# First weight tiles begun from the third attention group on, and Fourier constants queued behind the second batch's local loads

## The chip, the cores and the metric

The kernel runs on one NeuronCore of a Trainium2 chip. The metric is the device time of one execution in microseconds (us); the number for a kernel is the median of its runs. An engine executes its own instructions in order and waits on semaphores for other engines and for DMA transfers. PE is the matrix engine, DVE the vector engine, ACT the scalar engine, POOL is GpSimd, and SP only issues transfers here.

## The reference

```python
attn_out = _attn_ref(q, k, v)              # 4 batches, 8 heads, 576 positions, 64 wide; masks local and strided
x = attn_out.transpose(0, 2, 1, 3).reshape(B, S, H * D)
# first layer
mixed = real(fft(fft(x, axis=1), axis=2))
u = x + mixed
un = (u - mean(u)) / sqrt(var(u) + 1e-6)
x = u + relu(un @ w_ch1) @ w_ch2           # 512 -> 2048 -> 512
# second layer: over tokens, then over channels
u = x + (relu(x.T @ w_tok1) @ w_tok2).T    # 576 -> 256 -> 576
out = u + relu(u @ w_ch1) @ w_ch2          # 512 -> 1536 -> 512
```

The weights come as 64-bit floats.

## The kernel before, in words

**Stages.** Attention of four batches; a Fourier transform of each batch as matrix products with cosine and sine tables (`Fourier`, L254); the first MLP (`Mlp`, matmuls at L379 and L397); the token mixing; the last MLP (L777 and L807). Matrix operands are split into a high and a low part, and a product is three matmuls.

**Attention groups.** `gl` holds 24 groups, numbered by `gno`: six per batch, first three local ones (`gi` 0 to 2), then three strided ones (`gi` 3 to 5). A group's steps are `scores` (mask matmul L175, then q·k at L181, into a bank `sc`), `softmax` (DVE maximum L197, ACT scaling L198, ACT exponentials L200 into `sm`), `trans` (PE transposes L208, ACT copy L210 into `pt`), `av` (L223), and `out` (DVE, then SP writes to `xd` at L243, or L249 and L250).

**Loads of a batch.** q lies in `qz` and k in `k`, one buffer each for the local half (`qz_114`) and the strided half (`qz_115`); v lies in `vl` and `vs`. Batch 0 is loaded from SP. Later batches are loaded from POOL's queue (`bulk`, L142): at `gi == 3` the next batch's local q, k and `vl` (L533, L534), at `gi == 0` the strided q, k and `vs` (L536, L537). A buffer is filled again when the last group of the batch before has read it.

**Constants.** The cosine and sine tables `cs`, `ss`, `cd`, `sd` and `alt` are 13 transfers from POOL's queue (L489 to L493, about 1.7 MB). In the kernel before, a memset (`tick`, L481) waits until `vs` of batch 0 has landed, and the 13 issues follow it.

**Weights.** `load_wa` (L505) takes the next tile of the list `order`: w1 of block 0, w2 of block 0, w1 of block 1 and so on. A tile is a 512 KB load by SP into one of three `wraw` buffers (L86), an ACT step (L90), four DVE steps (L92 to L95) that make 32-bit floats of the 64-bit ones, the high part by ACT (L100) and the low part by POOL (L101). The attention loop calls it eight times. The names below write `wu`, `wAh` and `wAl` for the results.

**Order.** The program is written in the order of the loop, and a list scheduler places every instruction on its engine by the time at which it thinks the operands are there; a call of `load_wa` at a later group can so stand earlier in the queues, and a change of one call moves many neighbours. `tc.issue_after(x)` keeps instructions of a block behind `x` on its engine. Transfers that POOL issues count on eight semaphores in turn (`DMASW0` to `DMASW7`): the ninth waits until the first has landed, and so on.

Of the kernel before, what the change touches and what calls it, by code (L numbers as in the profile page):

```python
# [37 lines left out]
def f32(ap):  # L38
    return ap.bitcast(F32)
# [3 lines left out]
def attention_fourier_mlp_kernel(ctx: ExitStack, tc: tile.TileContext, a: dict, out: bass.AP):  # L43
    nc = tc.nc
# [91 lines left out]
    v_t = {}  # L136

    def bulk(b):
        return nc.gpsimd if b else nc.sync

    def load_qk(b, g, pool):
        t = pool.tile([P, 2, S], F32, tag=f"k{g}", name="k", bufs=(1, 1)[g])  # L142
        k_t[b, g] = t
        for ps in ([slice(0, 1), slice(1, 2)] if b == 0 and g < 1 else [slice(0, 2)]):
            for e in range(2):
                r = slice(64 * e, 64 * e + 64)
                bulk(b).dma_start(out=qz[g][r, e, ps], in_=a["qt"][b, g, r, ps])
            bulk(b).dma_start(out=t[:, ps], in_=a["kt"][b, g, :, ps])

    def load_vl(b):  # L150
        bulk(b).dma_start(out=v_t["l"], in_=a["vl"][b])

    def load_vs(b):
        return bulk(b).dma_start(out=v_t["s"], in_=a["vs"][b])
# [255 lines left out]
    def u_rows(T, u):  # L410
        for p0, n, b, r0 in spans(T):
            nc.sync.dma_start(out=u[p0:p0 + n], in_=ud[b][r0:r0 + n, :])
        return u
# [5 lines left out]
    def ln_stats(us, pool, prev=None):  # L419
        n = len(us)  # L420
        mv = pool.tile([P, 3, 4], F32, tag="mv", name="mv", bufs=2)
        for i, u in enumerate(us):
            st = pool.tile([P, 6], F32, tag="bs", name="bs", bufs=2)
            behind(nc.vector.bn_stats(out=st, in_=u), prev)
            nc.vector.bn_aggr(out=mv[:, i, 0:2], in_=st)
        behind(nc.scalar.activation(out=mv[:, :n, 2], in_=mv[:, :n, 1], func=AF.Sqrt, bias=eps), gl[-1].exp)
        nc.vector.reciprocal(out=mv[:, :n, 3], in_=mv[:, :n, 2])
        nc.vector.scalar_tensor_tensor(out=mv[:, :n, 2], in0=mv[:, :n, 0], scalar=-1.0, in1=mv[:, :n, 3],
                                       op0=ALU.mult, op1=ALU.mult)
        return [mv[:, i] for i in range(n)]  # L430
# [9 lines left out]
    if True:  # L440
# [23 lines left out]
        for g in range(2):  # L464
            for hp in range(2):
                nc.vector.memset(qz[g][64:128, 0, hp], 0.0)
                nc.vector.memset(qz[g][0:64, 1, hp], 0.0)
        load_vl(0)
        load_qk(0, 1, ap)
        vlast = load_vs(0)  # L470
        for b in range(B):
            nc.sync.dma_start(out=xd[b][S // 2:S // 2 + 1], in_=zero)

        cs = [fp.tile([P, 3, 290], F32R, name=f"cs{i}") for i in range(2)]
        ss = [fp.tile([P, 3, 290], F32R, name=f"ss{i}") for i in range(2)]
        cd = [fp.tile([P, 2, 258], F32R, name=f"cd{i}") for i in range(2)]
        sd = [fp.tile([P, 2, 258], F32R, name=f"sd{i}") for i in range(2)]
        alt = fp.tile([P, 258], F32R, name="alt")
        f = fp.tile([P, 2, 3, 512], F32R, name="f")
        g4 = [fp.tile([P, 290], F32R, name=f"g4{x}") for x in "hl"]  # L480
        tick = nc.gpsimd.memset(f32(g4[0]), 0.0)  # L481
        tc.add_manual_dep(tick.ins, vlast.ins.name, mybir.DependencyInfo(mybir.DependencyClass.Sync, mybir.DependencyReason.DATA), reason="constants behind the first batch")
        for t in (g4[1], alt, f[:, 0, 2], f[:, 1, 2], cs[0][:, 2], cs[1][:, 2], ss[0][:, 2], ss[1][:, 2]):
            nc.gpsimd.memset(f32(t), 0.0)
        cons = tc.issue_after(tick.ins)
        cons.__enter__()
        for i in range(2):
            for t, w in ((cs[i], a["cs"][i]), (ss[i], a["ss"][i])):
                nc.gpsimd.dma_start(out=t[:, 0:2], in_=w[:, 0:2])  # L489
                nc.gpsimd.dma_start(out=t[:33, 2], in_=w[:33, 2])  # L490
            nc.gpsimd.dma_start(out=cd[i], in_=a["cd"][i])
            nc.gpsimd.dma_start(out=sd[i], in_=a["sd"][i])
        nc.gpsimd.dma_start(out=alt[:2], in_=a["alt"])  # L493
        cons.__exit__(None, None, None)

        fst2 = ExitStack()
        fq = fst2.enter_context(tc.tile_pool(name="fft2", bufs=1, side="left"))
# [7 lines left out]
        def load_wa():  # L505
            if order:
                x, f = order.pop(0)
                pool, tag = (wa, "wa") if f < 4 else (wx, "wx") if f < 8 else (wb, "wb") if f < 12 else (wc, "wc")
                (w1 if x == "1" else w2)[f] = slot_w(a["w1a" if x == "1" else "w2a"][f], pool, tag, "wA")

        def fft(b):

            four_b, n = four[b], 6 * (b + 1)
            d = 1 if b == 0 else 0
            for i in range(3):
                g, e = divmod(7 + d + i, 2)
                yield n + g, lambda i=i, p=(n + g, e): four_b.prep(i, group(*p, "red"))
            for mt in range(5):
                p = (n + 5 + (mt + d) // 2, (mt + d) % 2)
                yield p[0], lambda mt=mt, p=p: four_b.s1(mt, group(*p, "mm"))  # L520
            for i in range(3):
                p = (n + 7 + (i + d + 1) // 2, (i + d + 1) % 2)
                yield p[0], lambda i=i, p=p: four_b.s2(i, group(*p, "mm"))
# [6 lines left out]
        for gno, g in enumerate(gl):  # L530
            b, gi = g.b, g.gi
            if gi == 3 and b + 1 < B:
                load_qk(b + 1, 0, ap)  # L533
                load_vl(b + 1)  # L534
            if gi == 0 and b > 0:
                load_qk(b, 1, ap)  # L536
                load_vs(b)  # L537
            g.scores()
            for e in range(2):
                g.softmax(e)  # L540
            for e in range(2):
                g.trans(e)
            for e in range(2):
                g.av(e)
                g.out(e)
            if gi == 2 and b > 0:
                for i in range(3):
                    four[b - 1].load(i)
                slices += fft(b - 1)
            while slices and slices[0][0] <= gno:  # L550
                slices.pop(0)[1]()
            if gno == 19:
                us = [u_rows(T, lp.tile([P, DM], F32, tag="u", name="u", bufs=6)) for T in range(3)]
            if gno == 23:
                mvs = ln_stats(us, lp, gl[21].red[1])
            if gno >= 8 and gno % 2 == 0:
                load_wa()
        for _, piece in slices:
            piece()
# [410 lines left out]
```

## Time and profile before

| | |
|---|---|
| median of 3 runs | 956.71 us (955.11 to 959.26) |
| the profiled execution | 954.82 us, span of its instructions 953.0 us |
| busy: PE, PEld, DVE, ACT, POOL | 97%, 89%, 57%, 39%, 23% of the span |
| matmuls | 6094 |
| moved by DMA | 113.86 MB, mean 119 GB/s |
| granted TensorE clock, mean | 0.994 of full speed |

A row of a timeline has the start in us, the duration in us, engine, line, operation, the tile written and read, the shape, and in brackets the idle time of the engine before it with what ended it. PEld is the loading of weights into PE, which overlaps PE. The attention of the four batches takes about the first 150 us.

### The profile page before, as it was taken

How to read it: one execution, taken by the hardware profiler on the slowest of the kernel's cores; microseconds unless marked ns; L12 is line 12 of the kernel's file. 1: busy time of each engine (PE TensorE's matmuls, PEld its weight loads, DVE VectorE, ACT ScalarE, POOL GpSimd, SP SyncE). 2: the span in 40 equal slices, each digit the busy share in tenths (PEclk: the TensorE clock that was granted, in tenths of full speed). 3: DMA queues.
4: the chain of work that ended last, by engine and by line, in shares of the span. 5: the costliest groups of instructions: out<-in, count | busy, mean ns of one | idle time of the engine just before them, and what ended most of it. 6: DMA issues, size and time to landing. Idle time of an engine off the chain costs nothing.

```text
span 953.0 us, 16043 instructions
## 1 busy us (share of the span) xinstructions
PE 922.9 (97%) x6094; PEld 851.4 (89%) x6094; DVE 543.5 (57%) x1183; ACT 375.0 (39%) x998; POOL 219.1 (23%) x246
## 2 busy tenths in 40 slices
PE   7889998999999999999999999999999999999997
PEld 6779998998888978898999988779999999999997
DVE  6777877899865645312212677544545545554554
ACT  5887776434433334112112445212333333333332
POOL 3442312333444344000000667342000000000000
PEclk9989999999999999999999999999999999999999
DMA  9998752354446756200200454499011101100000
GB/s 291 317 278 251 219 167 87 127 161 133 155 121 194 243 171 189 89 1 1 67 1 1 149 149 161 126 294 293 2 45 45 35 12 45 46 23 24 23 23 23
DMA packets 73352, 113.86 MB, mean 119 GB/s; under 512 B 6862, under 2 KB 39476, under 8 KB 73276
## 3 DMA queue, kind: packets, MB, share of 16 engines
q1 hardware_dynamic: 62572, 87.73, 29.1%
q0 software_dynamic: 10448, 24.90, 9.5%
q8 instruction: 48, 0.79, 0.3%
q14 instruction: 28, 0.23, 0.1%
q10 hardware_dynamic: 256, 0.21, 0.1%
HBM read 78.98 MB, written 33.83 MB: 118 GB/s over the span
## 4 chain that ended last, share of the span: by engine, by line
PE 55%; POOL 2%; DVE 1%; issue 1%; DMA 1%; ACT 0%; DVEq 0%; POOLq 0%; SPq 0%; ACTq 0%
PE h L777 16%; PE oo L807 14%; PE oo L397 9%; PE h L379 9%; PE tk L704 3%; PE tu L724 3%; POOL wu L92 1%; PE ut L762 1%; DMA wraw<-in_w1b_dram 1%; POOL w1bl L101 0%; PE ut L365 0%; DVE u L831 0%; DVE wu L94 0%; DVE wu L95 0%; POOL wtl L101 0%
## 5 line engine op out<-in xcount | busy, mean ns | idle before, releaser
L807 PE MATMUL oo<-w2b,hh 128*128 128x256 f32 x756 | 140.4, 284 | 0.0
L379 PE MATMUL h<-uth,wAh 128*128 128x384 f32 x384 | 130.1, 340 | 0.0
L379 PE MATMUL h<-utl,wAh 128*128 128x384 f32 x384 | 129.6, 338 | 0.0
L379 PE MATMUL h<-uth,wAl 128*128 128x384 f32 x384 | 129.6, 338 | 0.0
L384 DVE SCALAR_TENSOR_TENSOR hl<-h,hh 128x384 fp32r<-128x384 f32 x96 | 52.6, 551 | 120.2 <-ACT hh L383 120.2
L777 PE MATMUL h<-uth,w1bl 128*128 128x256 f32 x432 | 121.0, 280 | 0.0
L777 PE MATMUL h<-utl,w1bh 128*128 128x256 f32 x432 | 120.9, 280 | 0.0
L777 PE MATMUL h<-uth,w1bh 128*128 128x256 f32 x432 | 120.8, 280 | 0.0
L397 PE MATMUL oo<-wAh,hh 128*128 128x512 f32 x288 | 114.5, 400 | 5.8 <-ACT hh L383 2.9
L807 PEld LDWEIGHTS oo<-w2b,hh 128*128 128x128 f32 x756 | 116.2, 189 | 0.0
L397 PE MATMUL oo<-wAl,hh 128*128 128x512 f32 x288 | 113.5, 394 | 0.0
L397 PE MATMUL oo<-wAh,hl 128*128 128x512 f32 x288 | 106.4, 397 | 1.2 <-DVE hl L384 1.1
L807 PE MATMUL oo<-w2b,hl 128*128 128x256 f32 x378 | 104.5, 282 | 0.0
L789 DVE TENSOR_TENSOR hz<-hw 128x128 f32<-128x128 f32 x108 | 26.5, 287 | 114.0 <-ACT hw L783 114.0
L383 ACT ACTIVATE hh<-h 128x384 fp32r<-128x384 f32 x96 | 45.8, 483 | 115.4 <-PE h L379 115.4
L783 ACT ACTIVATE hw<-h 128x512 f32<-128x512 f32 x54 | 32.3, 598 | 148.1 <-PE h L777 135.9
L777 PEld LDWEIGHTS h<-uth,w1bh 128*128 128x128 f32 x432 | 81.3, 188 | 0.2
L777 PEld LDWEIGHTS h<-utl,w1bh 128*128 128x128 f32 x432 | 81.3, 188 | 0.1
L777 PEld LDWEIGHTS h<-uth,w1bl 128*128 128x128 f32 x432 | 81.3, 188 | 0.1
L379 PEld LDWEIGHTS h<-uth,wAl 128*128 128x128 f32 x384 | 72.2, 188 | 2.9
L379 PEld LDWEIGHTS h<-utl,wAh 128*128 128x128 f32 x384 | 72.2, 188 | 2.3
L379 PEld LDWEIGHTS h<-uth,wAh 128*128 128x128 f32 x384 | 72.1, 188 | 1.9
(169 smaller groups left out, 1894.8 us busy)
## 6 DMA issues: line engine op xcount, KB each, us to landing
w2b<-wsd POOLq DMA_DIRECT2D x42, 256.0 KB, 5.7
wraw<-in_w1a_dram SPq DMA_DIRECT2D x16, 512.0 KB
wraw<-in_w2a_dram SPq DMA_DIRECT2D x16, 512.0 KB
wraw<-in_w2b_dram SPq DMA_DIRECT2D x48, 128.0 KB
wraw<-in_w1b_dram SPq DMA_DIRECT2D x12, 512.0 KB
wsd<-wbh SPq DMA_DIRECT2D x12, 448.0 KB
wsd<-wbl SPq DMA_DIRECT2D x12, 448.0 KB
out_dram<-u SPq DMA_DIRECT2D x16, 256.0 KB
```

Of the source, the lines that this page charges most:

```text
L92: eng.tensor_scalar(f32(u), f32(u), E_MIN, E_MAX, op0=ALU.max, op1=ALU.min)
L379: nc.tensor.matmul(out=h[:, :384], lhsT=l[:, ws], rhs=r[:, kd, :], start=x == 0, stop=x == 11)
L383: nc.scalar.activation(out=hh, in_=h[:, :384], func=AF.Relu)
L384: nc.vector.scalar_tensor_tensor(out=hl, in0=h[:, :384], scalar=0.0, in1=f32(hh), op0=ALU.max, op1=ALU.subtract)
L397: nc.tensor.matmul(out=self.o[c][i], lhsT=l[:, s], rhs=r, start=first and x == 0, stop=last and x == 2)
L704: nc.tensor.matmul(out=hp[m], lhsT=wt1(w, t, m)[q], rhs=r[q], start=t == 0 and x == 0, stop=t == 4 and x == 2)
L724: nc.tensor.matmul(out=o[:q0 + n], lhsT=wt2(w, k, 128 * t - q0, q0 + n), rhs=r, start=k == 0 and x == 0, stop=k == 1 and x == 2)
L762: nc.tensor.transpose(tp[:, kd * P:(kd + 1) * P], u2[T][:, kd * P:(kd + 1) * P], ident)
L777: nc.tensor.matmul(out=h[:, 256 * i:256 * i + 256], lhsT=l[:, ws], rhs=r[:, kd, 0:256], start=x == 0, stop=x == 11)
L783: nc.scalar.activation(out=w, in_=h, func=AF.Relu)
L789: nc.vector.tensor_tensor(out=o, in0=x, in1=y, op=op)
L807: ends.append(nc.tensor.matmul(out=acc[c][bank][:, 256 * half:256 * half + 256], lhsT=lh[:, s], rhs=r, start=m == 0 and x == 0 and half == ...
```

## The change

Eight calls of `load_wa` are still made, but at `gno` 2, 5, 8, ..., 23 in place of 8, 10, ..., 22. The constants are no longer behind `tick`; they are issued right behind `vl` of batch 1, at `gno` 3.

```diff
     def load_vl(b):
-        bulk(b).dma_start(out=v_t["l"], in_=a["vl"][b])
+        return bulk(b).dma_start(out=v_t["l"], in_=a["vl"][b])
...
-        tick = nc.gpsimd.memset(f32(g4[0]), 0.0)
-        tc.add_manual_dep(tick.ins, vlast.ins.name, mybir.DependencyInfo(mybir.DependencyClass.Sync, mybir.DependencyReason.DATA), reason="constants behind the first batch")
-        for t in (g4[1], alt, f[:, 0, 2], f[:, 1, 2], cs[0][:, 2], cs[1][:, 2], ss[0][:, 2], ss[1][:, 2]):
+        for t in (g4[0], g4[1], alt, f[:, 0, 2], f[:, 1, 2], cs[0][:, 2], cs[1][:, 2], ss[0][:, 2], ss[1][:, 2]):
             nc.gpsimd.memset(f32(t), 0.0)
-        cons = tc.issue_after(tick.ins)
-        cons.__enter__()
-        for i in range(2):
...
-        cons.__exit__(None, None, None)
+
+        def constants():
+            for i in range(2):
...
             if gi == 3 and b + 1 < B:
                 load_qk(b + 1, 0, ap)
-                load_vl(b + 1)
+                last = load_vl(b + 1)
+                if b == 0:
+                    with tc.issue_after(last.ins):
+                        constants()
...
-            if gno >= 8 and gno % 2 == 0:
+            if gno >= 2 and (gno - 2) % 3 == 0:
                 load_wa()
```

On POOL, before, the queue from the first constant to the strided loads of batch 1 (`qz_114`, `k` and `vl` are its local loads, `qz_115` and the second `k` its strided ones):

```order
L481 MEMSET g4h 128x290
L489 DMA cs_142<-in_cs_dram 128x580
...
L493 DMA alt<-in_alt_dram 2x258
L147 DMA qz_114<-in_qt_dram 64x1152 x2
L148 DMA k<-in_kt_dram 128x1152
L101 ISA
L101 TENSOR_TENSOR wAl<-wu,wAh 128x512 x2
L151 DMA vl<-in_vl_dram 128x1536
L147 DMA qz_115<-in_qt_dram 64x1152 x2
L148 DMA k<-in_kt_dram 128x1152
```

and now, with the semaphores that the rows wait for:

```order
L148 DMA k<-in_kt_dram 128x1152 [waits DMAHW7_49,DMAHW4_49]
L101 ISA
L101 TENSOR_TENSOR wAl<-wu,wAh 128x512 [waits Activation_49] x2
L151 DMA vl<-in_vl_dram 128x1536 [waits DMAHW0_49,PE_49]
L487 DMA cs_142<-in_cs_dram 128x580
...
L488 DMA cs_143<-in_cs_dram 33x290 [waits DMASW5_49]
...
L491 DMA alt<-in_alt_dram 2x258 [waits DMASW2_49]
L147 DMA qz_115<-in_qt_dram 64x1152 [waits DMAHW1_49,DMASW3_49,PE_49]
L147 DMA qz_115<-in_qt_dram 64x1152 [waits DMAHW2_49,DMASW4_49,PE_49]
L148 DMA k<-in_kt_dram 128x1152 [waits DMAHW3_49,DMASW5_49]
```

The 13 constants moved from ahead of batch 1's local loads to between its local and its strided loads. `DMASW5` at `cs_143` was last raised by `vl`, and at the last `k` by that `cs_143` row.

On SP, before, from the fifth weight load on (L243, L249 and L250 write batch 0's attention):

```order
L86 DMA wraw<-in_w1a_dram 128x1024
L243 DMA xd_69<-x 96x2x256
L249 DMA xd_69<-x 9x7x256
...
L250 DMA xd_69<-x 9x6x256
L86 DMA wraw<-in_w2a_dram 128x1024
L249 DMA xd_69<-x 9x6x256
L250 DMA xd_69<-x 9x6x256
L86 DMA wraw<-in_w1a_dram 128x1024
```

and now:

```order
L86 DMA wraw<-in_w1a_dram 128x1024
L243 DMA xd_69<-x 96x2x256
L86 DMA wraw<-in_w2a_dram 128x1024
L249 DMA xd_69<-x 9x7x256
...
L250 DMA xd_69<-x 9x7x256
L86 DMA wraw<-in_w1a_dram 128x1024
L249 DMA xd_69<-x 9x6x256
```

The sixth load moved ahead of eight writes, the seventh ahead of six.

On DVE, before, the maxima of the second batch's last local score bank (96x4) and of its first strided ones (126x4), with conversions of the fifth and sixth tiles between them:

```order
L93 TENSOR_SCALAR wu<-wu 128x512
L197 TENSOR_REDUCE st<-sc 96x4
L232 TENSOR_SCALAR st<-st 96x8
L94 SCALAR_TENSOR_TENSOR wu<-wraw,wu 128x512
L233 RECIPROCAL st<-st 96x8
L197 TENSOR_REDUCE st<-sc 126x4
L95 SCALAR_TENSOR_TENSOR wu<-wraw,wu 128x512
L197 TENSOR_REDUCE st<-sc 126x4
```

and now:

```order
L92 TENSOR_SCALAR wu<-wu 128x512
L93 TENSOR_SCALAR wu<-wu 128x512
L92 TENSOR_SCALAR wu<-wu 128x512
L94 SCALAR_TENSOR_TENSOR wu<-wraw,wu 128x512
L234 TENSOR_TENSOR x<-av,st 96x512
L93 TENSOR_SCALAR wu<-wu 128x512
L95 SCALAR_TENSOR_TENSOR wu<-wraw,wu 128x512
L94 SCALAR_TENSOR_TENSOR wu<-wraw,wu 128x512
L95 SCALAR_TENSOR_TENSOR wu<-wraw,wu 128x512
L197 TENSOR_REDUCE st<-sc 126x4 x2
```

All eight conversion steps of the fifth and sixth tiles now stand after the last local maximum and ahead of the first strided one; the third and fourth tiles moved the other way, to ahead of batch 1's first maximum.

## Rows read from the trace of the kernel before

**Rows 1.** Windows: stretch, length; PE, PEld, DVE, ACT, POOL busy; clock; DMA share; GB/s.

```profile
0.00:25.00 25.00, 18.81 (x137) 16.63 (x138) 15.54 (x32) 15.41 (x71) 10.32 (x26) 1.00 1.02 296
25.00:50.00 25.00, 20.74 (x180) 18.25 (x178) 18.25 (x37) 18.80 (x87) 12.14 (x17) 1.00 1.06 306
50.00:75.00 25.00, 23.04 (x174) 21.27 (x175) 21.59 (x46) 22.52 (x98) 11.79 (x10) 0.86 0.98 280
...
100.00:125.00 25.00, 24.80 (x217) 23.46 (x216) 18.32 (x42) 20.47 (x99) 8.01 (x7) 1.00 0.77 226
...
152.00:400.00 248.00, 241.66 (x1262) 215.86 (x1261) 170.99 (x321) 96.12 (x185) 92.39 (x101) 0.99 0.51 157
```

**Rows 2.** Timeline of PE, 17 to 52 us.

```profile
17.58 1.04 PE L181 MATMUL sc<-k,qz 128*96 128x128 f32 x8
...
37.70 2.42 PE L181 MATMUL sc<-k,qz 128*96 128x128 f32 x20 [2.16 <-DMA k<-in_kt_dram]
...
51.21 1.34 PE L208 MATMUL tp<-ident_r,sm 96*128 96x96 f32 x4 [2.69 <-ACT sm L200]
```

**Rows 3.** Timeline of POOL, 17 to 34 us.

```profile
17.95 0.57 POOL L489 DMA_DIRECT2D cs<-in_cs_dram  x1
...
25.73 0.51 POOL L493 DMA_DIRECT2D alt<-in_alt_dram  x1
...
28.00 0.54 POOL L148 DMA_DIRECT2D k<-in_kt_dram  x1
...
31.09 0.57 POOL L151 DMA_DIRECT2D vl<-in_vl_dram  x1
...
33.06 0.56 POOL L148 DMA_DIRECT2D k<-in_kt_dram  x1
```

**Rows 4.** Timeline of ACT, 28 to 59 us.

```profile
28.90 0.35 ACT L198 ACTIVATE st<-st 108x4 f32<-108x4 f32 x2
...
50.15 0.66 ACT L90 ACTIVATE wu<-wraw 128x512 f32<-128x512 f32 x1 [2.91 <-DMA wraw<-in_w2a_dram]
...
58.30 0.36 ACT L200 ACTIVATE sm<-sc,st 126x126 f32<-126x126 f32 x1
```

**Rows 5.** Windows behind PE's second wait, columns as in group 1.

```profile
52.00:56.00 4.00, 3.96 (x24) 3.75 (x25) 3.53 (x7) 3.11 (x16) 1.26 (x1) 0.65 1.05 236
56.00:60.00 4.00, 4.00 (x40) 3.88 (x40) 1.98 (x5) 4.00 (x20) 1.27 (x1) 0.92 1.03 367
```

**Rows 6.** Groups by line, ACT, 28 to 58 us (busy us, mean ns | idle before).

```profile
L210 ACT ACTIVATE pt<-tp 128x384 f32<-128x384 f32 (+3 forms) x10 | 4.8, 492 | 0.9 <-PE tp L208 0.9
L90 ACT ACTIVATE wu<-wraw 128x512 f32<-128x512 f32 x4 | 2.7, 670 | 2.9 <-DMA wraw<-in_w2a_dram 2.9
L100 ACT ACTIVATE wAh<-wu 128x512 fp32r<-128x512 f32 x4 | 2.5, 634 | 0.3 <-DVE wu L95 0.3
L198 ACT ACTIVATE st<-st 96x4 f32<-96x4 f32 (+3 forms) x11 | 2.1, 232 | 3.0 <-DVE st L197 3.0
```

**Rows 7.** Groups by line, DVE, 28 to 58 us.

```profile
L197 DVE TENSOR_REDUCE st<-sc 96x4 f32<-96x512 f32 (+3 forms) x11 | 6.7, 611 | 3.5 <-PE sc L181 3.5
L95 DVE SCALAR_TENSOR_TENSOR wu<-wraw,wu 128x512 int32<-128x512 int32 x4 | 4.6, 1154 | 0.0
L94 DVE SCALAR_TENSOR_TENSOR wu<-wraw,wu 128x512 int32<-128x512 int32 x4 | 2.7, 680 | 0.0
L92 DVE TENSOR_SCALAR wu<-wu 128x512 f32<-128x512 f32 x4 | 2.2, 547 | 3.0 <-ACT wu L90 3.0
L93 DVE TENSOR_SCALAR wu<-wu 128x512 int32<-128x512 int32 x4 | 1.7, 421 | 0.0
```

**Rows 8.** DMA issues, 30 to 45 us: KB each, median us to landing.

```profile
k<-in_kt_dram POOLq DMA_DIRECT2D x1, 576.0 KB, 11.1
```

**Rows 9.** DMA issues, 0 to 75 us.

```profile
wraw<-in_w1a_dram SPq DMA_DIRECT2D x6, 512.0 KB
wraw<-in_w2a_dram SPq DMA_DIRECT2D x5, 512.0 KB
```

More of the change, by code (lines that the diff above doesn't have):

```diff
@@ L469, in attention_fourier_mlp_kernel @@
         load_qk(0, 1, ap)
-        vlast = load_vs(0)
+        load_vs(0)
         for b in range(B):
@@ L480, in attention_fourier_mlp_kernel @@
         g4 = [fp.tile([P, 290], F32R, name=f"g4{x}") for x in "hl"]
-        tick = nc.gpsimd.memset(f32(g4[0]), 0.0)
-        tc.add_manual_dep(tick.ins, vlast.ins.name, mybir.DependencyInfo(mybir.DependencyClass.Sync, mybir.DependencyReason.DATA), reason="constants behind the first batch")
-        for t in (g4[1], alt, f[:, 0, 2], f[:, 1, 2], cs[0][:, 2], cs[1][:, 2], ss[0][:, 2], ss[1][:, 2]):
+        for t in (g4[0], g4[1], alt, f[:, 0, 2], f[:, 1, 2], cs[0][:, 2], cs[1][:, 2], ss[0][:, 2], ss[1][:, 2]):
             nc.gpsimd.memset(f32(t), 0.0)
-        cons = tc.issue_after(tick.ins)
-        cons.__enter__()
-        for i in range(2):
[L488 to L493, printed above, removed]
-        cons.__exit__(None, None, None)
+        def constants():
+            for i in range(2):
+                for t, w in ((cs[i], a["cs"][i]), (ss[i], a["ss"][i])):
+                    nc.gpsimd.dma_start(out=t[:, 0:2], in_=w[:, 0:2])
+                    nc.gpsimd.dma_start(out=t[:33, 2], in_=w[:33, 2])
+                nc.gpsimd.dma_start(out=cd[i], in_=a["cd"][i])
+                nc.gpsimd.dma_start(out=sd[i], in_=a["sd"][i])
+            nc.gpsimd.dma_start(out=alt[:2], in_=a["alt"])
         fst2 = ExitStack()
```

## The prediction, made before the changed kernel ran

> **What bounds the kernel now.** I read the page's busy shares first: PE works 97% of the span, so a change pays only where PE stands still or runs slowly. The windows then say where that is [rows 1]. In the first 75 us PE is busy for 18.81, 20.74 and 23.04 of 25 us; the first of these holds the start-up, which the change does not touch. From 25 to 75 us PE idles 4.3 + 2.0 = 6.2 us, and from 50 to 75 us it was granted 0.86 of its clock on the mean. From 152 to 400 us it idles 248.00 - 241.66 = 6.3 us in all, in small pieces. So the place is 25 to 75 us, the passage from batch 0 to batch 1.
>
> PE's timeline names the two large waits [rows 2]. At 37.70 us the first scores of batch 1 had waited 2.16 us for k. At 51.21 us a transpose had waited 2.69 us for ACT's exponentials. The second is not ACT's own doing: ACT stood for 2.91 us in front of L90, a weight step, until the sixth weight tile had landed at 50.15 us [rows 4], and the exponentials were queued behind it.  After that wait PE's clock was 0.65 of full speed over 4 us and 0.92 over the next four [rows 5]: the granted clock lay at 1.2 GHz for a part of that stretch, and what came before it was the wait of 2.69 us. The lost work is 0.35 x 4 + 0.08 x 4 = 1.7 us.
>
> **The change part by part.** *Constants out of the way.* Before, POOL issues the 13 constants from 17.95 us to 25.73 + 0.51 = 26.24 us, and k of batch 1 only at 28.00 us [rows 3]; it lands when PE's wait ends, at 37.70 us, 9.7 us later. The buffers are free earlier: the last local scores of batch 0 run from 17.58 us to 18.62 us [rows 2]. With two q issues ahead of it of about 0.55 us each (as the POOL rows show for such issues), k goes out near 19.7 us, and with the same 9.7 us it is there at 29.4 us. PE was ready for it at 37.70 - 2.16 = 35.5 us. The first wait goes whole: **-2.16 us** on PE.
>
> *Weights earlier.* The sixth load now stands ahead of eight attention writes in SP's queue, and its ACT step no longer stands among the local exponentials of batch 1. ACT's 2.91 us and PE's 2.69 us behind it go.
>
> *What is late next.* ACT is the engine to follow here. Between the scaling at 28.90 us and the first strided exponential of batch 1 at 58.30 us [rows 4] lie 29.4 us. In its groups the idle time in front of L198, L90, L210 and L100 adds up to 3.0 + 2.9 + 0.9 + 0.3 = 7.1 us [rows 6], so 22.3 us are work. Up to that same exponential the changed order has the same instructions, in another order. Without any wait ACT would be there at 28.9 + 22.3 = 51.2 us, a lead of 7.1 us. But the order puts the fifth and sixth tiles at the end of this stretch: both ACT steps L90, then on DVE all eight conversion steps, and only then the first strided maximum. ACT comes to the first L90 two L90 and two L100 earlier, at 51.2 - 2 x 0.67 - 2 x 0.63 = 48.6 us; the step ends at 49.3 us. DVE's eight steps take 2 x (0.55 + 0.42 + 0.68) plus two L95. An L95 has a mean of 1.15 us here [rows 7], but this mean mixes short ones with long ones; its work is L94's, two tensors of the same size, and I take L94's 0.68 us. That is 4.7 us, to 54.0 us; with the maximum of 0.61 us [rows 7] and the scaling of 0.23 us [rows 6] the exponential starts at 54.8 us. With the mean of L95 it is 55.7 us. I take the first, a lead of 58.3 - 54.8 = **3.5 us**, because POOL's subtractions of these two tiles come after DVE's steps and not beside them. So of the 7.1 us, 3.6 us are given back on DVE.
>
> *The constants' new place.* k for the strided half of batch 1 went out at 33.06 us, right behind `vl` at 31.09 us [rows 3]. Now 13 issues lie between them. They took 8.3 us from the first to the end of the last; `vl` can go out no later than before, so this k goes out by about 41.4 us. With the 11.1 us that it took before [rows 8] it is there at 52.5 us. Its scores then end before DVE is through with the conversions at 54.0 us. So this delay of 8.3 us costs nothing as long as those conversions cover it; without that cover ACT would have wanted these scores at 51.2 us, and the cost would be up to 2.2 us (52.5, the matmuls and the maximum, against 51.2 us). The tables themselves are first read after 65 us, when batch 0 has been written and read back, and nothing waits for them.
>
> *The clock.* PE will still stand near 50 us, waiting for the strided exponentials instead of the local ones. I count the 1.7 us of lost clock as unchanged; the bounds are 0 and the whole 1.7 us.
>
> *The rest of attention and later.* Eight tiles are converted in the attention loop as before, and the same number of matmuls runs. From 100 to 125 us PE is busy for 24.80 of 25 us [rows 1], so there a lead at 55 us is neither won nor lost. The scheduler has also reordered neighbours between 140 and 400 us. For their effect I have no row but the 6.3 us of idle time [rows 1]: half of it either way, 3 us, is my bound, and 0 my value.
>
> **Sum.** -3.5 us. The profiled execution took 954.82 us, which becomes 951.3 us; the median shown is 1.9 us above that execution, so I forecast 956.71 - 3.5 = **953.2 us**. The bounds: 7.1 + 1.7 = 8.8 us of gain (947.9 us) if both waits and the slow clock go and nothing comes in their place, and no gain, plus 2 us of the reordering, at 959 us.
>
> **The rivals.** *Full lead.* The two conversions slip in beside the exponentials, and the lead is 7.1 us without or with part of the clock: 956.7 - 7.9 = 948.8 us. For it: DVE is busy for only 18.25 of 25 us between 25 and 50 us [rows 1]. Against it: the eight steps stand in a row in DVE's queue.
>
> *The DMA engines take it back.* They are busy for 1.02, 1.06 and 0.98 of their time in the first three windows and move 25 x (296 + 306 + 280) = 22.0 MB by 75 us [rows 1]; moving transfers to another place in the queues frees none of that. If everything moved by 75 us were due by then, the lead would be gone: 956.5 us. But eleven weight loads of 512 KB are in it [rows 9], and the attention loop converts eight; three of them, 1.57 MB, could come later, 5.5 us of transfer at 280 to 306 GB/s, and that is more than 3.5 us. The Trainium skill, page "DMA: Bandwidth & Descriptors", section "Issuing engines are not separate DMA queues", says that transfers of scalar, sync and gpsimd all end on the same 16 DMA engines and interleave. By that rule alone this rival would hold, at 956.5 us; the trace agrees that the engines are full, at 1.02 to 1.06.
>
> *Slower.* The last constants wait for earlier landings on POOL's eight semaphores: the 33-partition piece of `cs_143` waits for `vl` of batch 1, and the strided k waits for that piece. If each landing takes the 11.1 us of [rows 8], then `vl` at 31.09 us lands at 42.2 us, the piece issued behind it at 42.7 + 11.1 = 53.8 us, and k at 64.9 us. With 1.5 us for scores, maximum and scaling the first strided exponential starts at 66.4 us in place of 58.3 us: 8.1 us slower, 964.8 us. The point from which it decides is k landing after 56.8 us. Against it: the pieces are small, and with less in front of them `vl` should land faster.
>
> *The weights do not move.* The scheduler had already pulled the first loads ahead of their calls; if the sixth load still arrives late, only the first wait goes, and half of it comes back on ACT: 955.6 us. Against it: the order shows that load eight writes earlier.
>
> **How the numbers follow.** My forecast of 953.2 us (its own range 950.5 to 955.8 us) has 0.47, the full lead 0.20, the DMA engines 0.20, slower 0.08, weights not moved 0.05. About 0.5% (4.8 us) is what a measurement of this kernel tells from no change, so faster means below 951.9 us: the full lead, and some 0.11 of the forecast's lower part, 0.31. Slower means above 961.5 us: 0.08. The rest, 0.61, is the same within 0.5%. The range of 948.0 to 959.0 us leaves out the slower rival and the tails of the others.
>
> **What would show it.** Right: the first scores of batch 1 follow the last work of batch 0 with no wait for k; no wait of ACT for a weight tile near 50 us; the eight conversion steps in a row on DVE near 50 to 54 us with PE idle some 2 us behind them; the first strided exponential of batch 1 near 54.8 us. Wrong: a PE wait for the strided k of batch 1 that ends after 56 us; that exponential at 58 us or later; or a lead at 60 us that is gone by 160 us.

## The result: 964 to 969 us, about 1% slower

The changed kernel took 968.71 us (median of 4 runs, 963.76 to 971.23) beside 957.32 us of the kernel before in runs of the same session: a ratio of 1.0113, 95% interval [1.0066, 1.0161]. In a second session it took 964.1 us (12 runs) beside 954.76 us (25 runs): 1.0081 [1.0053, 1.0109]. Both intervals lie above the 0.5% that the prediction called a difference. One long run of the twelve, and below one of eight with the constants alone, over 1.5% above the fastest of its kernel, counts in the median given but not in the ratio. The profiled execution took 969.79 us, its span is 968.0 us, 15.0 us more than the span before.

**Profile after.** Windows of the changed kernel, columns as in [rows 1], with the stretch from 75 to 100 us added:

```profile
0.00:25.00 25.00, 15.69 (x103) 13.89 (x103) 11.15 (x23) 10.45 (x45) 6.04 (x18) 0.99 0.96 246
25.00:50.00 25.00, 22.44 (x186) 20.70 (x187) 18.12 (x40) 22.97 (x109) 12.59 (x20) 0.88 0.89 270
50.00:75.00 25.00, 18.01 (x147) 16.34 (x146) 13.08 (x29) 15.57 (x67) 8.23 (x11) 0.86 1.02 249
75.00:100.00 25.00, 20.73 (x152) 19.33 (x153) 20.40 (x45) 17.77 (x82) 10.62 (x11) 0.80 0.71 212
100.00:125.00 25.00, 22.75 (x211) 21.95 (x210) 18.04 (x45) 16.97 (x76) 7.01 (x7) 1.00 0.75 243
152.00:400.00 248.00, 241.84 (x1290) 216.03 (x1289) 176.54 (x349) 107.79 (x227) 90.97 (x103) 0.99 0.49 151
```

Count what PE lost in a window as its idle time plus window length times (1 - clock). After, the first four windows lose 9.3 + 0.3, 2.6 + 3.0, 7.0 + 3.5 and 4.3 + 5.0, 34.9 us together. Before, three of them stand in [rows 1], and the fourth is:

```profile
75.00:100.00 25.00, 24.04 (x221) 23.22 (x220) 19.21 (x44) 18.56 (x83) 4.46 (x8) 1.00 0.81 231
```

These four lose 6.2, 4.3, 2.0 + 3.5 and 1.0, 16.9 us. So 18 us more are lost by 100 us, and some of it is given back later. From 152 to 400 us PE idles 6.2 us after and 6.3 us before: nothing happened there. The DMA column is the one to read next: 246, 270 and 249 GB/s stand where [rows 1] has 296, 306 and 280.

**The two waits that the forecast removed are gone, and others have come.** PE's timeline:

```profile
41.23 1.04 PE L181 MATMUL sc<-k,qz 128*96 128x128 f32 x8
...
61.18 4.75 PE L181 MATMUL sc<-k,qz 128*126 128x126 f32 x24 [3.19 <-DMA k<-in_kt_dram]
...
74.89 0.53 PE L300 MATMUL g<-cs,f 128*128 128x290 f32 x2 [3.31 <-ACT f L283]
...
80.14 0.42 PE L208 MATMUL tp<-ident_r,sm 108*108 108x108 f32 x1 [3.03 <-ACT sm L200]
```

Batch 1's first local scores at 41.23 us wait for nothing; in [rows 2] they had waited 2.16 us. Its first strided scores wait 3.19 us for k, and the first Fourier products and a transpose stand 3.31 and 3.03 us. ACT's timeline:

```profile
22.21 0.66 ACT L90 ACTIVATE wu<-wraw 128x512 f32<-128x512 f32 x1 [3.14 <-DMA wraw<-in_w1a_dram]
...
25.59 0.66 ACT L90 ACTIVATE wu<-wraw 128x512 f32<-128x512 f32 x1 [2.33 <-DMA wraw<-in_w2a_dram]
...
64.22 0.37 ACT L200 ACTIVATE sm<-sc,st 126x126 f32<-126x126 f32 x1
```

The wait for the sixth weight tile [rows 4] is gone, but the first and the second tile are waited for, 3.14 and 2.33 us, inside batch 0. The first strided exponential of batch 1 starts at 64.22 us, 5.9 us later than before and 9.4 us later than forecast.

**Where the transfers went.** POOL's timeline, to be laid beside [rows 3]:

```profile
17.00 0.55 POOL L147 DMA_DIRECT2D qz<-in_qt_dram  x1 [11.52 <-PE sc L181]
19.77 0.53 POOL L147 DMA_DIRECT2D qz<-in_qt_dram  x1 [2.22 <-PE tp L208]
20.29 0.55 POOL L148 DMA_DIRECT2D k<-in_kt_dram  x1
31.98 1.30 POOL L101 TENSOR_TENSOR wAl<-wu,wAh 128x512 fp32r<-128x512 f32 x1 [11.14 <-ACT st L198]
34.57 1.27 POOL L101 TENSOR_TENSOR wAl<-wu,wAh 128x512 fp32r<-128x512 f32 x1 [1.29 <-ACT wAh L100]
35.78 0.57 POOL L151 DMA_DIRECT2D vl<-in_vl_dram  x1
36.34 0.54 POOL L487 DMA_DIRECT2D cs<-in_cs_dram  x1
...
44.33 0.52 POOL L491 DMA_DIRECT2D alt<-in_alt_dram  x1
...
48.45 0.52 POOL L147 DMA_DIRECT2D qz<-in_qt_dram  x1 [2.07 <-PE av L223]
48.96 0.55 POOL L148 DMA_DIRECT2D k<-in_kt_dram  x1
```

From 20.84 to 35.78 us POOL issues nothing. Two subtractions of weight tiles stand ahead of `vl` and wait for ACT, and `vl` itself could not have gone out sooner than 35.42 us, when PE's last product with batch 0's `vl` freed the buffer:

```profile
34.61 0.81 PE L223 MATMUL av<-vl,pt 128*96 128x64 f32 x8
```

The 13 constants follow from 36.34 us on, strided k at 48.96 us. Windows of 4 us show what that does to the DMA engines:

```profile
28.00:32.00 4.00, 4.00 (x28) 3.92 (x28) 2.66 (x5) 3.99 (x22) 0.02 (x1) 0.60 0.53 174
32.00:36.00 4.00, 4.00 (x41) 3.87 (x41) 3.67 (x7) 2.63 (x10) 2.71 (x3) 1.00 0.46 113
```

They are busy for half their time (0.53, 0.46), in a kernel that before kept them full (0.98 to 1.06) for its first 75 us. Afterwards they are full (1.02 from 50 to 75 us), and what is due lands late. SP writes the last piece of batch 0's attention and then reads it back for the Fourier part:

```profile
50.19 0.75 SPq L250 DMA_DIRECT2D xd<-x  x1
61.81 0.34 SPq L264 DMA_DIRECT2D xa<-xd  x1
```

The read could start 10.9 us after that write ended, and DVE, in order, stood in front of the first Fourier step with batch 1's maxima behind it:

```profile
72.33 0.69 DVE L278 TENSOR_TENSOR w<-xa,xr 128x510 f32<-128x510 f32 x1 [5.08 <-DMA xr<-xd]
```

Before, the last write was issued at 44.41 us, the read at 51.32 us, 6.2 us after that write ended, and this DVE step ran at 60.69 us without a wait for its inputs (SP's timeline, then DVE's):

```profile
44.41 0.75 SPq L250 DMA_DIRECT2D xd<-x  x1
51.32 0.33 SPq L264 DMA_DIRECT2D xa<-xd  x1
60.69 0.69 DVE L278 TENSOR_TENSOR w<-xa,xr 128x510 f32<-128x510 f32 x1
```

### The profile page after: what moved, and what is told of

Read it like the earlier page. It is cut to its first block, busy times and chain, and to the rows that moved or that the text cites. A ratio compares the mean times of both kernels' runs of the same rounds, so it can differ in the third digit from the quotient of the medians.

```text
span 968.0 us, 16036 instructions
## 1 busy us (share of the span) xinstructions
PE 928.0 (96%) x6094; PEld 856.4 (88%) x6094; DVE 538.7 (56%) x1183; ACT 375.8 (39%) x998; POOL 213.5 (22%) x246
## 4 chain that ended last, share of the span: by engine, by line
PE 54%; DMA 2%; DVE 1%; issue 1%; POOL 0%; ACT 0%; SPq 0%; DVEq 0%; POOLq 0%; ACTq 0%
PE h L777 16%; PE oo L807 14%; PE oo L397 9%; PE h L379 8%; PE tk L704 3%; PE tu L724 3%; PE ut L762 1%; DMA cr<-x2d 1%; DMA x2d<-v 1%; POOL wu L92 0%; DMA v<-ud 0%; PE ut L365 0%; DVE wu L94 0%; DVE u L831 0%; DVE hl L384 0%
```

## The experiments

Theories: **V**, the slow start belongs to the execution profiled. **D**, batch 1's local q and k, out at 17 to 20 us, slow the first weight tiles. **W**, the earlier weight conversions cost the time. **Q**, strided k behind 13 issues in POOL's queue. From the first four runs came **B**, the bytes of the constants on full DMA engines, against **S**, the order that the scheduler gives. **G**, **N** and **F** are stated with the runs that they were made for. Medians of 6 to 12 runs; the kernel before had 17 to 35 beside each group, with medians of 954.76 us beside the first four rows, 957.1 beside the next four, 956.79 beside the next two, 957.58 beside the next three and 955.61 beside the last two. The ratios are estimates over all runs of a group and not quotients of two medians: for the constants alone that quotient is 1.013.

| kernel | median, us | ratio to before, 95% interval |
|---|---|---|
| the change again | 964.1 | 1.0081 [1.0053, 1.0109] |
| weights alone | 956.45 | 1.0019 [0.9993, 1.0044] |
| constants alone | 967.16 | 1.0098 [1.0064, 1.0133] |
| constants behind strided k | 974.13 | 1.0173 [1.0131, 1.0215] |
| constants behind local k | 958.62 | 1.0011 [0.9981, 1.0040] |
| the same, old weight groups | 955.48 | 0.9981 [0.9951, 1.0012] |
| q, k held | 961.64 | 1.0051 [1.0021, 1.0081] |
| no constants | 956.69 | 0.9973 [0.9941, 1.0006] |
| q, k held, constants behind k | 958.56 | 1.0012 [0.9981, 1.0044] |
| the same, old weight groups | 956.04 | 0.9985 [0.9957, 1.0013] |
| 13 issues, few bytes | 956.37 | 0.9991 [0.9962, 1.0021] |
| constants behind vs | 959.16 | 1.0026 [1.0000, 1.0052] |
| the same, q, k held, old groups | 956.28 | 0.9990 [0.9965, 1.0014] |
| the change, Fourier later | 968.72 | 1.0125 [1.0091, 1.0159] |
| before, Fourier later | 963.26 | 1.0072 [1.0050, 1.0093] |

### The two halves, and the change again

> The changed kernel once more, nothing edited, for a second profile of its first 28 us. Theory V (the slow start belongs to the execution profiled, not to the change: between 12 and 16 us, where no engine's order differs, the DMA engines moved 249 GB/s against 312 before): the first conversion of a weight tile on ScalarE starts near 19 us as before, its wait is under 1 us, and the first strided exponential of batch 1 comes 4 to 6 us earlier than 64.2. Theory D (batch 1's local q and k, issued at 17.0 to 20.3 us instead of 26.8 to 28.0, slow the first weight tiles): that conversion starts near 22 us again and waits about 3 us, the second about 2 us. Both theories: median 964 to 971 us.

> The weight tiles' new groups alone; constants where they were. Theory Q (strided k of batch 1, behind vl and 13 constant issues in GpSimd's queue, is what is late) and theory D: no loss, 952 to 957 us; strided k issued near 33 us, and PE does not wait for it. Theory W (the earlier weight tiles' conversions themselves delay the attention steps): slower by 5 us or more, 960 to 966 us, with the first strided exponential of batch 1 later than 58.3 us.

> The constants' new place alone; weight tiles in their old groups. Theory Q: strided k issued after 45 us and PE waiting over 2 us for it near 58 us, 962 to 970 us. Theory D: a wait of over 2 us for the first weight tile on ScalarE near 19 to 22 us, 960 to 966 us. Theory W: as before, 955 to 959 us.

The first has no edit. The second is the kernel before with one line of the change, the third is the change without it:

```diff
-            if gno >= 8 and gno % 2 == 0:
+            if gno >= 2 and (gno - 2) % 3 == 0:
                 load_wa()
```

The constants alone cost as much as the whole change, 1.0098; the weights alone cost nothing that is measured. W falls. The constants-alone profile took 959.79 us, the shortest of that kernel's runs, so its trace shows less than its median; it has the same signs:

```profile
43.06 0.55 POOL L148 DMA_DIRECT2D k<-in_kt_dram  x1
```

```profile
44.27 0.75 SPq L250 DMA_DIRECT2D xd<-x  x1
56.89 0.34 SPq L264 DMA_DIRECT2D xa<-xd  x1
```

Strided k goes out at 43.06 us (the first row, POOL's timeline) and the Fourier read 11.9 us behind the last write (SP's timeline). In the change's second profile the first weight tile is waited for 5.62 us and the second 2.81 us. So the slow start was no matter of that one execution; D had about 3 and 2 us, and the first wait is larger.

### The strided loads ahead of the constants

> The whole change, but the 13 constant issues stand behind batch 1's strided q and k instead of ahead of them. Theory Q: strided k issued by 41 us and landed by 53, PE's 3.2 us wait for it gone, first strided exponential of batch 1 at 55 to 59 us where it was 64.2, 953 to 960 us. Theory D: the start is still 5 to 6 us late at 28 us and the time stays at 961 to 968 us. Theory W: 963 to 971 us, as the whole change.

```diff
             if gi == 0 and b > 0:
-                load_qk(b, 1, ap)
+                last = load_qk(b, 1, ap)
+                if b == 1:
+                    with tc.issue_after(last.ins):
+                        constants()
                 load_vs(b)
```

Slowest of all, outside every theory's numbers. Q was right in its own place: PE's waits from 28 to 100 us name no k, and the first strided exponential comes at 58.41 us. But `vs` now stands behind the constants and goes out at 58.70 us, and the Fourier inputs come later still. DVE, then PE, in their timelines:

```profile
77.21 0.69 DVE L279 TENSOR_TENSOR w<-xa,xr 128x510 f32<-128x510 f32 x1 [15.81 <-DMA xr<-xd]
```

```profile
81.27 0.97 PE L209 MATMUL tp<-ident_r,sm 108*108 108x108 f32 x4 [14.10 <-DVE x L235]
```

A wait of 3.2 us for k was exchanged for one of 14.1 us. In this kernel what stood behind the constants, or shared the engines with them, was the next thing late.

### The constants before vl, and without bytes

> The whole change, but the 13 constant issues follow batch 1's local k directly instead of its vl, which GpSimd can only issue when batch 0's last local weighted sums are done. Theory B (what costs is that the constants wait behind vl: the DMA engines are half idle at 28 to 36 us, share 0.53 and 0.46, and afterwards carry 2.3 MB of constants together with strided k, vs and batch 0's stores, which all land 10 to 12 us after issue): DMA share over 0.9 at 28 to 36 us, strided k of batch 1 issued before 42 us, PE's wait for it under 1 us, the Fourier input's load waits under 5 us for the stores instead of 10.7, and 15 to 17 us from batch 1's first strided exponential to batch 2's first local one instead of 22.9: 950 to 958 us. Theory S (the order that the scheduler gives ScalarE, VectorE and GpSimd in the changed kernel costs the time, wherever the bytes go): 962 to 970 us, that stretch still over 20 us.

```diff
-                load_qk(b + 1, 0, ap)
-                last = load_vl(b + 1)
+                last = load_qk(b + 1, 0, ap)
                 if b == 0:
                     with tc.issue_after(last.ins):
                         constants()
+                load_vl(b + 1)
```

(`load_qk` returns its last issue here and above.)

> The whole change with the 13 constant loads left out: the constants are set to zero on GpSimd in the first 17 us, when it has nothing else, so the Fourier part's output is zero. Theory B: with these bytes and issues gone strided k is issued before 42 us and lands within 10 us, the Fourier input's load waits under 5 us for the stores, 15 to 17 us from batch 1's first strided exponential to batch 2's first local one, and 947 to 956 us. Theory S: 961 us or more. Theory D: the wait for the second weight tile stays at 2 to 3 us.

```diff
-                last = load_vl(b + 1)
-                if b == 0:
-                    with tc.issue_after(last.ins):
-                        constants()
+                load_vl(b + 1)
```

> The whole change with its 13 constant issues in their place, but each loads 4 rows (2 for the last) in place of 128 or 33, some 80 KB in all in place of 2.3 MB; the rest of the constants is set to zero on GpSimd in the first 17 us, so the Fourier part's output is wrong. Issue theory (what costs is the 13 issues, some 0.55 us each, standing ahead of strided k and vs in GpSimd's queue): strided k still issued after 44 us, first strided exponential of batch 1 after 60 us less what the start gives, over 20 us from it to batch 2's first local one, 961 to 966 us. Byte theory (2.3 MB on DMA engines that are full, which strided k, vs, batch 0's stores and the Fourier inputs then share, and the issues' waits for one another's landings): Fourier input's load waits under 5 us for the stores, under 18 us in that stretch, 953 to 958 us, like the kernel without the loads.

```diff
-                    nc.gpsimd.dma_start(out=t[:, 0:2], in_=w[:, 0:2])
-                    nc.gpsimd.dma_start(out=t[:33, 2], in_=w[:33, 2])
+                    nc.gpsimd.dma_start(out=t[:4, 0:2], in_=w[:4, 0:2])
+                    nc.gpsimd.dma_start(out=t[:4, 2], in_=w[:4, 2])
...
```

The loss goes in all three; S falls. With the constants behind local k the same windows read:

```profile
28.00:32.00 4.00, 4.00 (x25) 3.94 (x25) 1.75 (x4) 2.40 (x9) 2.35 (x5) 0.50 1.22 372
32.00:36.00 4.00, 4.00 (x34) 3.94 (x33) 2.01 (x5) 2.55 (x14) 3.74 (x5) 0.77 1.14 380
```

372 and 380 GB/s in place of 174 and 113. `vl` goes out at 35.57 us, no later than in the change, strided k at 39.79 us in place of 48.96; the Fourier read waited 4.7 us for the writes, as B had it (under 5); it went out 5.9 us after the last write had ended, against 10.9 in the change. From the first strided exponential of batch 1 to the first local one of batch 2 it took 17.2 us (B: 15 to 17), where the change took 22.9.

The run with few bytes tells issues from bytes. Its 13 issues stand where the change has them, and strided k is as late in POOL's timeline:

```profile
38.76 0.57 POOL L151 DMA_DIRECT2D vl<-in_vl_dram  x1 [2.38 <-PE av L223]
...
48.26 0.57 POOL L148 DMA_DIRECT2D k<-in_kt_dram  x1
```

PE does not wait for it all the same, and the median is that of the kernel before. This profile had a slow start (3.90 and 3.12 us for the first two tiles) and took 962.31 us, the longest of its runs; its Fourier read still waited 11.9 us, which theory B had under 5. From the first strided exponential of batch 1 to the first local one of batch 2 it took 17.1 us, as B had it (under 18). So the place in the queue alone is worth nothing that is measured, while the times of the runs say that the bytes are needed for the loss.

The half-idle stretch from 28 to 36 us is not the loss by itself. Without the constants the engines were busy 0.50 of it, with few bytes 0.38, and neither kernel is slower; with the constants alone they were busy 0.88 of it, and that kernel is. Nor, as far as these profiles tell, is the read's long wait for the writes: it was 11.9 us with few bytes, and 10.0 us with q and k held and the constants behind k, in an execution of 958.47 us in a kernel that is no slower than before. What is shown is that the 2.3 MB in this place of the queue make the loss, not through which one wait.

The run without constants gives about the upper end of what a new place for them could win: 0.9973, at most 0.6%.

### The constants behind everything of batch 1

> The whole change, but the 13 constant issues stand behind batch 1's last load (vs) in GpSimd's queue. Byte theory: strided k is issued before 42 us and vs before 50, batch 0's stores and the Fourier inputs are shared with the constants from about 48 us on, and batch 2's local q and k come behind them: the loss moves to the Fourier inputs and to batch 2's k, 957 to 965 us. Issue theory: only what stands behind the 13 issues is late, batch 2's local q and k, which have slack: 953 to 958 us.

```diff
             if gi == 0 and b > 0:
                 load_qk(b, 1, ap)
-                load_vs(b)
+                last = load_vs(b)
+                if b == 1:
+                    with tc.issue_after(last.ins):
+                        constants()
```

959.16 us lies where the byte theory had it and outside the issue theory's 953 to 958, but the two ranges touch. What the place does to the transfers is in the profile: strided k is out at 36.39 us and `vs` at 43.69; the constants follow to 54.19 us, and the Fourier inputs share the engines with them. The waits of DVE, 46 to 90 us (total, times, longest), and PE's timeline:

```profile
DVE w L278 <- DMA xr<-xd: 9.8, 2, 5.5
```

```profile
62.78 1.94 PE L223 MATMUL av<-vs,pt 126*126 126x64 f32 x8 [5.36 <-ACT f L283]
```

This execution took 955.89 us, near the shortest of its kernel's runs and under the median of the kernel before, so these waits cost it nothing that its time shows. The bytes alone, with nothing of batch 1 behind them, cost 0 to 5 us; the issues alone cost nothing measured; both together cost some 9 us by the ratio.

### What batch 1's early q and k do to the start

> The whole change, but batch 1's local q and k wait until batch 0's vs has landed, as the constants' first memset made them before. Theory D (q and k issued from 16 us on slow the second weight tile): ScalarE's wait for the second weight tile falls from 2.3 to 2.8 us to under 0.7, the start is 2 us earlier at 28 us, and the time 1 to 3 us shorter than the change's 964: 961 to 963 us. Theory V (the start's DMA rate differs from execution to execution whatever the order): the wait for the first weight tile is anywhere between 0.5 and 6 us, no gain, 963 to 968 us. Theory B: both are minor, the loss after 56 us stays.

```diff
+        tick = nc.gpsimd.memset(f32(g4[0]), 0.0)
+        tc.add_manual_dep(tick.ins, vlast.ins.name, ...)
...
+                if b == 0:
+                    with tc.issue_after(tick.ins):
+                        load_qk(b + 1, 0, ap)
```

> The kernel before once more, nothing edited, for a second profile of its start. Theory V (the DMA rate of the start differs from execution to execution): anywhere from 230 to 310 GB/s at 12 to 16 us, and ScalarE's wait for the first weight tile anywhere from 0.5 to 5 us. Theory G (the slow start belongs to the weight tiles' new groups: the three profiles with the old groups had 289 to 312 GB/s there, the seven with the new ones 232 to 283): 289 GB/s or more, wait under 1.4 us.

> The weight tiles' new groups alone, a second profile. Theory V: 230 to 310 GB/s at 12 to 16 us, and if it is over 285 the start is as fast as the kernel before's. Theory G: under 285 GB/s and a wait of 1.7 us or more for the first weight tile.

With q and k held, ACT's timeline has:

```profile
22.06 0.66 ACT L90 ACTIVATE wu<-wraw 128x512 f32<-128x512 f32 x1 [3.13 <-DMA wraw<-in_w1a_dram]
23.28 0.69 ACT L90 ACTIVATE wu<-wraw 128x512 f32<-128x512 f32 x1 [0.17 <-DMA wraw<-in_w2a_dram]
```

Two waits, two causes. The second tile's is D's: over the 19 profiles of this study it is 0.17 to 0.88 us in the nine whose q and k go out behind `vs` of batch 0, and 0.54 to 3.12 us in the ten where they go out at 16 to 20 us. The first tile's wait is 0.47 to 3.65 us in the nine and 0.91 to 6.45 us in the ten: it varies with the execution, as V has it, and q and k may add to it. What holding is worth in time, 1.0051 against 1.0081, lies within the intervals. Theory G (a slow start belongs to the new weight groups) is not settled: between 12 and 16 us the seven profiles with the old groups moved 283 to 312 GB/s, the twelve with the new ones 232 to 304, with the same order of transfers up to there.

The second profile of the kernel before is the most telling of the controls:

```profile
0.00:28.00 28.00, 20.27 (x126) 17.74 (x127) 15.07 (x30) 16.26 (x75) 11.60 (x29) 0.91 1.00 282
28.00:40.00 12.00, 11.99 (x93) 11.19 (x91) 7.02 (x14) 8.53 (x40) 6.18 (x9) 0.78 1.05 333
40.00:60.00 20.00, 19.13 (x159) 16.31 (x158) 17.37 (x36) 17.61 (x81) 7.69 (x8) 1.00 0.94 263
60.00:80.00 20.00, 19.02 (x151) 17.33 (x149) 17.99 (x40) 17.11 (x72) 11.37 (x10) 0.91 0.88 281
```

The first profile of that kernel, in the same four windows, was busy for 21.81, 9.66, 16.74 and 18.42 us at clocks of 1.00, 1.00, 0.91 and 0.91:

```profile
0.00:28.00 28.00, 21.81 (x166) 19.57 (x166) 17.40 (x36) 18.41 (x82) 12.42 (x30) 1.00 1.03 301
28.00:40.00 12.00, 9.66 (x84) 8.46 (x84) 8.43 (x19) 8.90 (x44) 5.16 (x8) 1.00 1.07 321
40.00:60.00 20.00, 16.74 (x134) 14.87 (x133) 14.62 (x27) 15.87 (x75) 7.42 (x8) 0.91 1.04 281
60.00:80.00 20.00, 18.42 (x148) 16.99 (x146) 19.89 (x41) 16.78 (x69) 11.59 (x10) 0.91 0.83 248
```

The first lost 6.2 us by 28 us and 10.8 us from 28 to 80 us, 17.0 in all. The second lost 10.2 and 6.3 us, 16.5 in all, and both have a span of 953.0 us. In the second, neither wait of the forecast is there: PE's waits from 28 to 100 us name no k, and ACT's longest for a weight tile from 36 to 66 us is 0.5 us. And in the second profile of the weights alone, the wait that the new groups were to remove is there:

```profile
53.80 0.66 ACT L90 ACTIVATE wu<-wraw 128x512 f32<-128x512 f32 x1 [4.69 <-DMA wraw<-in_w2a_dram]
```

Counted in the same way, the two profiles of the weights alone lost 18.3 and 18.7 us by 80 us. In these two kernels, where a start with full DMA engines shows its waits differs from execution to execution; their sum hardly does.

### Arrangements that might beat both

> The same place for the constants, with the weight tiles in their old groups: what the weight tiles' new groups are worth where the constants do no harm. Theory B with a lead from the weight tiles: slower than the kernel with the new groups by 1 to 4 us. If the new groups are worth nothing in this kernel, as the run of them alone had it: the same within 2 us. Theory S: 962 to 970 us.

> Weight tiles in the new groups; batch 1's local q and k wait until batch 0's vs has landed, and the 13 constant issues follow that k directly, ahead of vl. Theory B together with D: no wait over 0.7 us for the second weight tile, strided k of batch 1 issued before 42 us, no wait of PE for local k (2.2 us before) nor for the sixth weight tile (2.7 us before): what the kernel before loses at 28 to 60 us should go, 950 to 955 us. Rival N (a lead at 60 us is not kept: the kernel without the constants' loads, which had the lead, measured like before): 954 to 958 us, the same as before.

> The same with the weight tiles in their old groups. If the new groups are worth their 3 us lead: 2 to 4 us slower than the kernel with them. Rival N: the same within 2 us, 953 to 958 us.

> Constants behind batch 1's vs, batch 1's local q and k held until batch 0's vs has landed, weight tiles in the old groups: the arrangement in which nothing urgent stands behind the constants until batch 2. Rival N (a lead at 60 us is not kept): 953 to 958 us, no gain over the kernel before. If the bytes of the constants are what the first 60 us have too many of: 948 to 953 us, faster than both.

These combine the edits above; "old groups" undoes the diff on `load_wa`. None beats the kernel before by more than the interval; the best ratio is 0.9981. With q and k held and the constants behind them, the first strided exponential of batch 1 comes at 50.39 us (new groups) and 50.21 us (old), 8 us ahead of [rows 4], but the first MLP's matmuls start at 157.9 and 153.0 us where before they started at 156.3, and from 200 to 400 us PE idles 7.8 and 9.4 us in place of 6.3. Rival N holds: a lead of 8 us at 50 us is not kept; with the old groups 3.3 us of it were left at 153.0 us, and PE's idle time up to 400 us took that too. Where the constants do no harm, the new groups measured 3.1 and 2.5 us above the old ones; both pairs overlap in their intervals, and neither shows the 3 us gain.

### The Fourier step on DVE

> The whole change, and batch 0's Fourier steps placed one attention group later in the program, so that two of batch 1's strided maxima and a weight conversion come out of the shadow of VectorE's first Fourier step, which stood 5.1 and 5.3 us for its inputs in the changed kernel's two profiles. Theory F (part of the loss goes through this place: the inputs are late, since batch 0's stores and reads share the DMA engines with the constants, and VectorE stands in front of them with attention steps behind it): that wait under 2 us, 958 to 962 us. If the loss is not there (strided k alone): 963 to 967 us, as the change.

> The same shift in the kernel before, where VectorE did not wait for the Fourier inputs: the control. Theory F: nothing to win, 954 to 959 us. If it gains 3 us or more here too, the shift is worth that by itself and says nothing on the loss.

```diff
-            d = 1 if b == 0 else 0
+            d = 3 if b == 0 else 0
```

The wait of DVE for the Fourier inputs is gone, and the time is no better, 968.72 us: in the profile, of the longest run (975.48 us), DVE stands 4.96 us for an attention write instead, ACT 4.1 us for a weight tile and PE up to 4.3 us behind ACT. The control costs 0.7% by itself, outside the 954 to 959 us of theory F. This pair did not isolate the DVE step's share; how the some 9 us divide between strided k and the Fourier inputs stays open.

## Why the prediction was wrong, step by step

- **The constants' new place, costed at 0.** This is the step that failed. It followed only strided k, and had it out "by about 41.4 us" and landed by 52.5; it went out at 48.96 us and was used from 61.18 us on. Of the 7.6 us, 4.7 are `vl`, which went out at 35.78 us and not "no later than before" (31.09 us): both the subtractions ahead of it and PE's last product with batch 0's `vl`, which ended at 35.42 us, came late, as ACT did. Some 3 us are waits of the two q issues (0.99 and 2.07 us). k itself took 12.2 us to its use in place of 11.1. The conversions did not cover it, as DVE's timeline shows: they ended at 61.86 us, not 54.0, and the first strided maximum still waited for its scores.

```profile
61.17 0.69 DVE L95 SCALAR_TENSOR_TENSOR wu<-wraw,wu 128x512 int32<-128x512 int32 x1
63.26 0.68 DVE L197 TENSOR_REDUCE st<-sc 126x4 f32<-126x504 f32 x1 [1.40 <-PE sc L181]
```

The larger omission is the bytes. "Nothing waits for them" is true of the tables, but batch 0's writes and the Fourier reads share the engines with them: the read waited to 61.81 us. Costed at 0, measured 9.4 us by the ratio (0.0098 of 954.76 us), and nothing with the same issues and few bytes. Through which of the waits the bytes cost it stays open.

- **Size of the constants.** The text ahead of the prediction has 1.7 MB. The DMA issues add up to 2 x (290 + 290 + 258 + 258 + 37.4 + 37.4) + 2 = 2344 KB, 2.3 MB: about 8 us at the 296 GB/s of [rows 1].
- **ACT's walk "from 28.90 us".** It was taken as unchanged up to there. ACT came to the same steps 5.7 us later: its first L100, before at 25.56 us, started at 31.25. q and k moved forward to 17.00 to 20.29 us, as forecast (19.7), and their cost to the weight tiles was not counted.
- **The first wait, -2.16 us.** Gone in this trace, as forecast, and so is ACT's wait near 50 us. But the second profile of the kernel before has neither wait, so this trace alone does not show that the change removed them.
- **A lead of 3.5 us from it.** Wrong: weights alone gave 1.0019, and the first strided exponential came at 60.45 and 62.66 us in its two profiles, not at 54.8. Taking away a wait that one execution shows was no gain. This was the rival "The DMA engines take it back". The objection to it was that three of eleven weight loads could come later; no run shows that they bought anything. By the Trainium skill's page "DMA: Bandwidth & Descriptors", section "Issuing engines are not separate DMA queues", starting transfers from several engines saves only the time of issuing them. The trace agrees for this half: the engines were busy 1.00 over the first 60 us in the weights-alone profile and 1.04 before.
- **The clock.** From 50 to 75 us the mean is 0.86 both times, as forecast, but by luck: after the change the clock is lowest from 60 to 64 us (0.50), behind PE's wait for strided k, which the forecast did not have. From 75 to 100 us it is 0.80, 5 us that were in no term: PE was busy for 0.53 us of the four from 72 to 76 and 0.61 us of the next four, and the granted clock was 0.50, the lower of its two levels, from 76 to 84 us.

```profile
76.00:80.00 4.00, 0.61 (x1) 0.29 (x1) 3.30 (x8) 1.51 (x7) 1.49 (x3) 0.50 1.06 333
80.00:84.00 4.00, 3.86 (x20) 3.71 (x21) 2.48 (x7) 3.84 (x18) 2.31 (x2) 0.50 0.83 267
```

- **Later reordering, 0 +- 3 us.** 152 to 400 us idles 6.2 us: right.
- **The rival "Slower", 964.8 us at 0.08.** Its point of decision was k landing after 56.8 us; k landed at 61.2 us, and the time was 964 to 969 us. Its working has too long a landing for `vl` (the piece of `cs_143` waited for it only until 41.31 us, 5.5 us after its issue, not 11.1) and too short a queue before it. The chance was too low, because the argument "the pieces are small" looked at the piece that waits and not at the 2.3 MB around it.

## What to carry to other kernels

Where the DMA engines are full, cost a moved transfer by its bytes and by the transfers that are then behind or beside it, not by its issue and its own due time; follow every transfer that is due in the next 15 us, writes and their read-backs too. Before moving issues behind an instruction, ask when that one can go out and whether the engines idle until then: here `vl` kept 2.3 MB back while the engines were half idle, and they then met the strided loads and batch 0's writes. The idle stretch alone cost nothing measured, as the kernel without constants had it too. And take a second profile of the unchanged kernel before pricing a wait: here two waits moved from execution to execution while the sum of PE's losses stayed, and a change made to remove one of them, the weights alone, was worth nothing.

## What the runs showed that was not expected

- The same transfers in the same order were moved at different rates: 232 to 312 GB/s between 12 and 16 us over 19 profiles, 283 and 312 for the unchanged kernel. ACT's first wait for a weight tile goes with it, 0.47 us at 312 GB/s, 5.62 at 232.
- A kernel without its 2.3 MB of constants (0.9973) and one with the strided exponentials 8 us earlier (1.0012, 0.9985) are no faster, though both profiles of the kernel before lose some 17 us on PE in the first 80. Nor does a loss in the first 100 us have to last: the profile without constants lost 22.7 us there, counted as above, 5.8 more than before, and its span is 954.0 us, 1.0 more.
- Thirteen issues of about 0.53 us each ahead of a load on POOL, 7 us and their waits, cost nothing measurable by themselves (0.9991 [0.9962, 1.0021]).
